# Sliding-window attention in 36 batches of four tiles that run across head groups, and column sums over partitions on GpSimd, in a gated mix of two attention blocks

## The chip, the cores and the metric

The kernel runs on one core of one Trainium2 chip. The metric is the device time of one execution in microseconds. Each run of a kernel has several executions; a median is quoted with the number of them. The profile is one execution of each kernel; its span is a little shorter than the measured time of the same execution (491.1 against 492.9 us for the kernel before).

Engine names: PE is the tensor engine (matmuls), PEld its weight loads, DVE is VectorE, ACT is ScalarE, POOL is GpSimd, SP issues most DMA; a q behind a name (SPq) is that engine's instruction queue. PSUM is the memory that the matmuls here write, bank by bank (a projection fills one bank with 128x512 fp32 values), and to evacuate a bank is to copy it to SBUF, where the program keeps its other tiles. The granted clock is the share of full speed that the profile shows for PE.

## The reference, cut to what matters

Two attention blocks read the same `x` (2048 x 1024, bf16), with 32 heads of 32, and a per-row gate mixes their outputs.

```python
# A: linear attention
pq, pk = phi(q), phi(k)                         # phi(t) = where(t > 0, t + 1, exp(t)) + 1e-6
kv = einsum("bhsd,bhse->bhde", pk, v)
z  = einsum("bhsd->bhd", pk)                    # column sums of A's keys over the 2048 rows
o  = einsum("bhqd,bhde->bhqe", pq, kv) / (einsum("bhqd,bhd->bhq", pq, z)[..., None] + 1e-6)
# B: each row attends to 8 keys, at distances 0, 2, ... 14
logits = where(mask, q . k[pos - 2 * w] * Dh ** -0.5, -1e9);  attn = softmax(logits)
# mix
g = sigmoid((x * gate_w).sum(-1));  out = g * A(x) + (1 - g) * B(x)
```

## The kernel before: the parts that the change and the argument touch

The rows are kept as even rows, then odd rows, so a distance of 2 becomes a distance of 1. In program order PE does: key projection of A (`pk_ps`); `G = x^T pk` (`g_ps`); `kv = Wv^T G` per head group (`kv_ps`) and the column sums (`z_ps`); value projection of B and query projection of A in turn (the "V stage", `p_ps`); then for each of 8 groups of four heads the key and query projection of B (`kq_ps`), with the window attention of the group before woven in; a rest of the query projection of A (`q_ps`); and the output projections (`q_ps`, `d_ps`). PE's order is the program's; the `interleave` helper sets the attention pieces between the projection matmuls.

Column sums: VectorE adds the 16 row tiles of `pk` into `zacc`, alternating with the 16 products for the gate; then `zacc` is split into a high and a low bf16 part, and matmuls with a matrix of ones sum both over the partitions.

```python
def side(t):                                   # called once per finished 128x512 piece of G
    if t:
        nc.vector.tensor_tensor(out=zacc[:], in0=zacc[:] if t > 1 else pk[:, 0, :], in1=pk[:, t, :], op=ALU.add)
    nc.vector.tensor_tensor_reduce(out=zhl[:, 0, :], in0=xrow[:, t, :], in1=gw_row[:], ..., accum_out=gdot[:, t:t + 1])
# [cut]
nc.vector.tensor_copy(out=zhl[:, 0, :], in_=zacc[:])
nc.vector.tensor_tensor(out=zhl[:, 1, :], in0=zacc[:], in1=zhl[:, 0, :], op=ALU.subtract)
# [cut: the kv matmuls]
for half in range(2):
    zp = ps_1.tile([P, 512], F32, name="z_ps", tag="p1")
    for i in range(2):
        nc.tensor.matmul(zp[:], lhsT=onesb[:], rhs=zhl[:, i, half * 512:(half + 1) * 512], start=(i == 0), stop=(i == 1))
    nc.scalar.copy(out=zrow[:, half * 512:(half + 1) * 512], in_=zp[:])
```

Window attention: the 2048 queries of a head group are 18 tiles of 112 or 128 queries, each against 128 keys. A batch is three or four tiles of one head group: 4, 4, 4, 3, 3 for seven groups, and six batches of three for the last, 41 in all. Scores use only the 32 rows of one head, so four heads run side by side as 32-row tiles.

```python
for q0, w, k0 in tiles:                        # scores of one batch
    for i in range(4):
        r = slice(32 * i, 32 * i + 32)
        nc.tensor.matmul(s4[:, i, o:o + w], lhsT=kqt[r, 0, k0:k0 + P], rhs=kqt[r, 1, q0:q0 + w], ...)
    o += w
for h in range(2):                             # two exponentials and two masks for a batch
    nc.scalar.activation(out=ptv[:, hs], in_=s4[:, hs, 0:W_], func=ACT.Exp, scale=SCALE)
    nc.vector.tensor_tensor(out=ptv[:, hs], in0=ptv[:, hs], in1=m[...], op=ALU.mult)
# later, after a lag: 4 value matmuls of 33 columns per tile, reciprocal, multiply, DMA transpose
```

## Time and profile before

| kernel before | value |
|---|---|
| time, median of 3 / of 6 executions | 493.66 us / 493.7 us |
| PE busy | 481.1 of 491.1 us |
| VectorE, ScalarE, GpSimd busy | 58%, 37%, 2% |
| 128x512 matmul: printed / real step | 379 ns / 0.216 us |

The first lines are from the page of the kernel before: the busy time of each engine with its share of the span and its number of instructions, and the shares of the chain that ended last by engine.

```profile
PE 481.1 (98%) x3276; PEld 230.0 (47%) x3336; DVE 282.8 (58%) x548; ACT 180.6 (37%) x279; POOL 7.6 (2%) x26
PE 91%; SPq 5%; DMA 2%; issue 1%; DVE 0%; ACT 0%; ACTq 0%
```

PE is almost always busy and almost the whole chain. What PE doesn't execute can only matter if PE waits for it. So PE's waits come next, for the kernel before: who waited for whom, us in total, times, the longest. "issue" stands for idle time in which the profile shows nothing that PE waited for.

```profile
PE kq_ps L338 <- issue: 1.3, 8, 0.2
PE warm L163 <- DVE onesb L116: 1.1, 1, 1.1
PE pk_ps L157 <- DMA WkA_75<-in_A_wqkv_dram: 0.7, 1, 0.7
PE pk_ps L157 <- DMA xT<-in_A_x_dram: 0.4, 1, 0.4
PE pk_ps L157 <- DMA WkA_96<-in_A_wqkv_dram: 0.3, 1, 0.3
PE q_ps L295 <- issue: 0.3, 2, 0.2
```

The third view is the PE timeline of the kernel before: start, duration, the instruction, its shapes and how many were merged. These lines are the boundaries: start of `kv_ps`, of the ones-matmuls, of the V stage, of attention and of the main output projection.

```profile
117.81 1.95 PE L220 MATMUL kv_ps<-G_624,WvA_102 128*128 128x128 bf16 x32
121.38 1.03 PE L227 MATMUL z_ps<-zhl,onesb 128*128 128x512 bf16 x3
122.25 1.03 PE L261 MATMUL p_ps<-WvB_110,xT 128*128 128x512 bf16 x4
222.39 1.89 PE L338 MATMUL kq_ps<-xT,WkB_1039 128*128 128x512 bf16 x8
384.23 1.89 PE L457 MATMUL d_ps<-WoA_106,pqT_4054 128*128 128x512 bf16 x8
```

A duration includes the tail of a pipelined matmul that overlaps the next, so one reads starts and not durations: from `z_ps` to `p_ps` is 0.87 us, which is four steps of 0.216 (only three of the four records are in the trace). From `kq_ps` to `d_ps`, the attention stretch, is 161.84 us.

### The profile page before, as it was taken

The numbers are of one execution on the slowest core, as the hardware profiler recorded it, in microseconds if no ns is written. First come the engines' busy times: TensorE is split into PE (matmuls) and PEld (weight loads), VectorE is DVE, ScalarE is ACT, GpSimd is POOL, SyncE is SP. The second block draws the span as 40 slices with busy tenths as digits, with TensorE's granted clock in tenths as the row PEclk, the third lists the DMA queues.
The fourth block names the chain that finished last, engine by engine and source line by source line (L and its number), as shares of the span: only waits on it lengthen the run. The fifth ranks groups of instructions, "written<-read, shape, count | busy, mean of one in ns | idle before, by whom it ended". The sixth has DMA issues, their size and how long they took to land.

```text
span 491.1 us, 8153 instructions
## 1 busy us (share of the span) xinstructions
PE 481.1 (98%) x3276; PEld 230.0 (47%) x3336; DVE 282.8 (58%) x548; ACT 180.6 (37%) x279; POOL 7.6 (2%) x26
## 2 busy tenths in 40 slices
PE   8999999999999999999999999999999999999997
PEld 5444444446444444444445444444544444444444
DVE  1666669951329999997476767676765496000000
ACT  2333321112543333332555555655565333112121
POOL 3000000000200000000000000000000000000000
PEclk9999999999999999999999999999999999999999
DMA  8999950001521222235011133111174933010101
GB/s 195 173 297 368 348 183 0 0 1 44 177 76 54 86 94 92 73 135 173 4 34 30 32 96 54 26 36 37 29 136 90 217 87 84 35 43 33 43 34 43
DMA packets 80309, 46.56 MB, mean 95 GB/s; under 512 B 53648, under 2 KB 74256, under 8 KB 80272
## 3 DMA queue, kind: packets, MB, share of 16 engines
q1 hardware_dynamic: 80272, 46.04, 34.4%
q8 instruction: 26, 0.43, 0.4%
q14 instruction: 11, 0.09, 0.1%
HBM read 21.23 MB, written 7.34 MB: 58 GB/s over the span
## 4 chain that ended last, share of the span: by engine, by line
PE 91%; SPq 5%; DMA 2%; issue 1%; DVE 0%; ACT 0%; ACTq 0%
PE kq_ps L338 23%; PE d_ps L457 21%; PE g_ps L202 11%; PE p_ps L261 11%; PE p_ps L295 8%; PE pk_ps L157 6%; SPq L104 4%; PE q_ps L295 2%; DMA WkA_96<-in_A_wqkv_dram 2%; PE kv_ps L220 1%; PE q_ps_4355 L457 1%; PE p_ps L250 1%; PE q_ps L457 1%; SPq L101 0%; PE q_ps_4236 L295 0%
## 5 line engine op out<-in xcount | busy, mean ns | idle before, releaser
L202 PE MATMUL g_ps<-pk,xrow 128*128 128x512 bf16 x251 | 55.2, 379 | 0.3
L145 DVE TENSOR_SCALAR e<-e 128x512 f32<-128x512 f32 x64 | 27.2, 425 | 42.7 <-ACT e L144 42.7
L462 ACT ACTIVATE osb<-d_ps,omg 128x512 bf16<-128x512 f32 (+1 forms) x31 | 20.9, 673 | 74.5 <-PE d_ps L457 68.7
L157 PEld LDWEIGHTS <-xT 128*128 128x128 bf16 x256 | 24.9, 98 | 32.5 <-issue 1.5
L457 PEld LDWEIGHTS <-OBT 128*128 128x128 bf16 x264 | 25.8, 98 | 29.2
L202 PEld LDWEIGHTS <-xrow 128*128 128x128 bf16 x256 | 25.0, 98 | 30.2
L261 PEld LDWEIGHTS <-xT 128*128 128x128 bf16 x256 | 25.0, 98 | 30.2
L295 PEld LDWEIGHTS <-xT 128*128 128x128 bf16 x256 | 24.2, 98 | 28.0
L144 ACT ACTIVATE e<-pk_ps 128x512 f32<-128x512 f32 x32 | 19.0, 597 | 42.3 <-PE pk_ps L157 33.2
L377 DVE TENSOR_TENSOR PT_1863<-PT_1863,mask 128x672 bf16<-128x672 bf16 (+3 forms) x42 | 23.7, 571 | 17.9 <-ACT PT_1863 L375 17.4
L338 PE MATMUL kq_ps<-xT,WqB_1846 128*128 128x512 bf16 x120 | 31.8, 379 | 1.0 <-issue 0.6
L338 PE MATMUL kq_ps<-xT,WqB_1844 128*128 128x512 bf16 x124 | 31.7, 379 | 0.7 <-issue 0.5
L377 DVE TENSOR_TENSOR PT_1864<-PT_1864,mask 128x672 bf16<-128x672 bf16 (+3 forms) x40 | 22.3, 565 | 17.0 <-ACT PT_1864 L375 16.5
L338 PE MATMUL kq_ps<-xT,WkB_1041 128*128 128x512 bf16 x122 | 31.6, 379 | 0.2
L344 DVE CAST kqt<-kq_ps 128x512 bf16<-128x512 f32 x32 | 22.0, 687 | 16.5 <-PE kq_ps L338 16.5
L338 PE MATMUL kq_ps<-xT,WkB_1039 128*128 128x512 bf16 x120 | 30.7, 379 | 0.4 <-issue 0.2
L261 PE MATMUL p_ps<-WvB_112,xT 128*128 128x512 bf16 x126 | 30.6, 379 | 0.1
L261 PE MATMUL p_ps<-WvB_110,xT 128*128 128x512 bf16 x125 | 30.6, 379 | 0.1
L266 ACT CAST tmp<-p_ps 128x512 bf16<-128x512 f32 x32 | 18.8, 588 | 30.2 <-PE p_ps L261 27.9
L457 PEld LDWEIGHTS <-pqT_4413 128*128 128x128 bf16 x200 | 19.6, 98 | 22.1
L157 PE MATMUL pk_ps<-WkA_75,xT 128*128 128x512 bf16 x125 | 28.1, 380 | 1.4 <-DMA WkA_75<-in_A_wqkv_dram 0.7
L457 PE MATMUL d_ps<-WoB_4050,OBT 128*128 128x512 bf16 (+1 forms) x126 | 28.3, 365 | 0.1
(393 smaller groups left out, 665.8 us busy)
## 6 DMA issues: line engine op xcount, KB each, us to landing
xrow<-in_A_x_dram SPq DMA_DIRECT2D x4, 1024.0 KB, 13.0
out_dram<-osb SPq DMA_DIRECT2D x31, 128.0 KB, 1.9
pqd<-tmp SPq DMA_DIRECT2D x12, 256.0 KB, 2.0
V<-tmp SPq DMA_DIRECT2D x4, 264.0 KB, 2.4
WkA_75<-in_A_wqkv_dram SPq DMA_DIRECT2D x4, 256.0 KB, 3.8
WkA_96<-in_A_wqkv_dram SPq DMA_DIRECT2D x1, 1024.0 KB, 8.5
WvA_102<-in_A_wqkv_dram SPq DMA_DIRECT2D x1, 1024.0 KB, 15.3
WvA_104<-in_A_wqkv_dram SPq DMA_DIRECT2D x1, 1024.0 KB, 14.7
```

Source lines behind the costliest of these rows:

```text
L104: nc.sync.dma_start_transpose(out=xT[:, :, t * P:(t + 1) * P], in_=rows(x, t * P, (t + 1) * P))
L144: nc.scalar.activation(out=e[:], in_=pj[:], func=ACT.Exp)
L145: nc.vector.tensor_scalar(out=e[:], in0=e[:], scalar1=1.0, scalar2=1e-6, op0=ALU.min, op1=ALU.add)
L157: nc.tensor.matmul(pj[:], lhsT=xT[:, kt, t * P:(t + 1) * P], rhs=WkA[half][:, kt, :], start=(kt == 0), stop=(kt == KT - 1))
L202: nc.tensor.matmul(pj[:], lhsT=xrow[:, t, kt * P:(kt + 1) * P], rhs=pk[:, t, half * 512:(half + 1) * 512], start=(t == 0), stop=(t == NB - 1))
L261: nc.tensor.matmul(st["pj"][:], lhsT=xT[:, kt, t * P:(t + 1) * P], rhs=WvB[half][:, kt, :], start=(kt == 0), stop=(kt == KT - 1))
L295: nc.tensor.matmul(st["pj"][:], lhsT=xT[:, kt, t * P:(t + 1) * P], rhs=WqA[half][:, kt, :], start=(kt == 0), stop=(kt == KT - 1))
L338: nc.tensor.matmul(st["pj"][:], lhsT=W[c // 4][:, kt, (c % 4) * P:(c % 4 + 1) * P], rhs=xT[:, kt, cols], start=(kt == 0), stop=(kt == KT - 1))
L344: nc.vector.tensor_copy(out=kqt[:, 1, cols], in_=st["pj"][:])
L377: nc.vector.tensor_tensor(out=ptv[:, hs], in0=ptv[:, hs], in1=m[:, None, :].broadcast_to([P, 2, W_]), op=ALU.mult)
L457: nc.tensor.matmul(st["ps"][:, 0:n], lhsT=lhsT, rhs=W[c0 // 512][:, c, c0 % 512:c0 % 512 + n], start=(side == 0 and c == 0), stop=(side == ...
L462: nc.scalar.activation(out=osb[:, 0:n], in_=st["ps"][:, 0:n], func=ACT.Copy, scale=omg[:, tb:tb + 1])
```

## The change

The intent: fewer and always equal attention batches, so that what a batch costs in itself is paid 36 times and not 41; and no PE work for the column sums. Supporting changes: the K or Q evacuation goes to VectorE when it falls just behind a batch's scores (ScalarE has exponentials to do then) and to ScalarE otherwise; VectorE does all adds first, so that the all-reduce can start early; and the projections in the last attention stretch lose a third PSUM bank, since each batch now needs both banks of the value matmuls.

```diff
-            def side(t):
-                if t:
-                    nc.vector.tensor_tensor(out=zacc[:], ... op=ALU.add)
-                nc.vector.tensor_tensor_reduce(out=zhl[:, 0, :], ... accum_out=gdot[:, t:t + 1])
+            side = []
+            for t in range(1, NB):
+                side.append(lambda t=t: nc.vector.tensor_tensor(out=zacc[:], ... op=ALU.add))
+            side.append(lambda: nc.gpsimd.partition_all_reduce(zrow[:], zacc[:], P, bass_isa.ReduceOp.add))
+            for t in range(NB):
+                side.append(lambda t=t: nc.vector.tensor_tensor_reduce(out=gjunk[:], ... accum_out=gdot[:, t:t + 1]))
 [cut: called two at a time; the bf16 split, the ones-matmuls and the zrow copies go]
-                        if which == 0:
-                            nc.scalar.copy(out=kqt[:, 0, cols], in_=st["pj"][:])
-                        else:
-                            nc.vector.tensor_copy(out=kqt[:, 1, cols], in_=st["pj"][:])
+                        after = (64 * c + 16 * b + 8 * which + 8 - 67) % (512 / 36)
+                        (nc.vector.tensor_copy if 0 <= after < 4 else nc.scalar.copy)(
+                            out=kqt[:, which, cols], in_=st["pj"][:])
-                GROUPS = [QT[a:b] for a, b in zip(cuts, cuts[1:])]      # batches within one head group
+            TILES = [(c, t) for c in range(KT) for t in range(18)]
+            state = [dict() for _ in range(len(TILES) // 4)]            # 36 batches across head groups
+            for g in range(len(state)):
+                p_ = 64 + 3 + 512 * g / len(state)
+                events.append((p_, lambda g=g: scores(g)))
+                events.append((p_ + 18, lambda g=g: pv(g)))
 [cut: masks for a 128-query tile in any place; bank8 (three banks) becomes bank2 (two)]
```

## The prediction

> **What bounds the kernel.** The tensor engine. The page gives PE 481.1 us busy of 491.1 (98%) at full granted clock; the chain of waits is 91% PE, and PE's own waits sum to about 4 us: 1.3 us "issue" in the K/Q projections, 1.1 us before the warm-up, 1.1 us for first loads, 0.3 us for the second half of Wk. VectorE has 58%, ScalarE 37%, GpSimd 2%. Only what PE executes, or a new wait, can count.
>
> **Terms on PE (PE timeline).** A 128x512 matmul advances the stream by 0.216 us (its printed 379 ns overlaps its neighbours).
> 1. Column sums: four ones-matmuls go (121.38 to 122.25): -0.87 us.
> 2. Batches: 41 (seven heads of 5, one of 6) become 36; the 144 tiles stay. The value part is linear in tiles (0.41 us for four, 0.31 for three): no gain. The score part takes about 0.39 us for four and 0.34 for three, so about 0.2 us of a batch is fixed: 5 x 0.2 = -1.0 us.
> 3. 0.16 us "issue" gaps recur behind some three-tile batches, some ten in all. Those batches vanish; I count half: -0.5 us.
> 4. In the last attention stretch projections have two PSUM banks, not three, all evacuated by ScalarE, whose pair of exponentials now always takes 1.8 us (1.35 for three tiles), where eight matmuls take 1.73. One or two short bank waits: +0.3 us.
>
> **Off the critical path.** Ten fewer exp and ten fewer mask instructions (fixed parts only, about 1.5 us on each engine), zrow copies (1.07 us ScalarE), the bf16 split of the sums (1.85 us VectorE). About 14 K/Q evacuations move from VectorE (0.69 us) to ScalarE (0.59 us). VectorE's busy time falls by some 13 us, ScalarE's rises by some 5; no effect on time.
>
> **The GpSimd sum.** The 15 VectorE adds, 1.14 us apart, now run first: 64.5 to 82 us. The all-reduce follows. Its result is first read at about 148 us, but GpSimd executes in order, and behind it stand two PT fills (1.66 us each) and the ones columns of V staging, which the first V transfers need at about 127 us and whose two buffers hold ScalarE from about 133. So about 45 us are free. The Trainium skill, "GPSIMD Engine Reference", Cross-partition, gives 247.7 us for a partition-axis reduce of 128x2048; by columns an estimated 124 us here, which would cost some 65 us. No run here shows it, and it is another instruction; I expect 10 to 40 us, hidden. The same page (Instruction dispatch) gives about 6 us for a routine's first call: hidden. Loading it adds DMA traffic in the first 35 us, where DMA is saturated and PE already waits for Wk: +0.3 us.
>
> **Sum.** -0.87 - 1.0 - 0.5 + 0.3 + 0.3 = -1.8 us: 491.9 us; 8 in 10 between 489.8 and 494.5. Chances: faster by over 2% 0.02, within 0.90, slower 0.08.
>
> **What would show it.** No z matmuls, V beginning 0.9 us sooner after G ends. 36 score batches; attention (first K/Q matmul to first d_ps matmul, 161.7 us before) about 160.5. PE waits still about 4 us, none on GpSimd; the first multiply by zrow not waiting for it. The all-reduce over before 125 us on the GpSimd timeline.
>
> **What would make it wrong.** An all-reduce over 50 us (GpSimd busy past 130 us, V transfers and ScalarE waiting, PE stalled for banks); early loads delayed by the routine's own transfer; bank or exponential waits at every batch (36 x 0.05 us would cancel everything).

## The result, and the profile after

The changed kernel took 491.62 us (median of 6, 490.83 to 492.64) against 493.7 us (median of 6, 492.6 to 494.39), ratio 0.9964 with a 95% interval of 0.9945 to 0.9983. A second set of 6 gave 491.2 us and 0.9962 (0.9947 to 0.9977). A ratio is the mean time of one kernel's fast runs over that of the other's of the same rounds, so it is not quite the ratio of the medians quoted. The gain is real and small: about 1.8 us, 0.4%.

The same lines of the page of the changed kernel:

```profile
PE 484.8 (99%) x3332; PEld 230.5 (47%) x3332; DVE 279.1 (57%) x512; ACT 188.4 (38%) x283; POOL 16.0 (3%) x33
PE 98%; DMA 1%; SPq 0%; ACT 0%; issue 0%; ACTq 0%
```

PE's busy time is higher although it does less: more of its records are in this trace (3332 matmul records against 3276, with four fewer executed). Busy time can't settle a change of 2 us here. PE's waits of the changed kernel and the boundaries from its PE timeline can:

```profile
PE warm L162 <- DVE onesb L114: 1.1, 1, 1.1
PE pk_ps L156 <- DMA WkA<-in_A_wqkv_dram: 0.9, 2, 0.7
PE pk_ps L156 <- DMA xT<-in_A_x_dram: 0.8, 1, 0.8
```

```profile
119.33 3.74 PE L220 MATMUL kv_ps<-G,WvA 128*128 128x128 bf16 x64
122.90 1.03 PE L254 MATMUL p_ps<-WvB,xT 128*128 128x512 bf16 x4
223.05 1.89 PE L331 MATMUL kq_ps<-xT,WkB 128*128 128x512 bf16 x8
383.82 1.89 PE L444 MATMUL d_ps<-WoA,pqT 128*128 128x512 bf16 x8
```

The differences of starts, for every profiled run (columns in us; "first" is from the first key projection to `g_ps`, read from the same view; "att" is the attention stretch; "output" is from the first `d_ps` to the end of the span, which is printed to 0.1 us):

| run | first | G | kv to V | V stage | att | output |
|---|---|---|---|---|---|---|
| before | 56.75 | 55.25 | 4.44 | 100.14 | 161.84 | 106.87 |
| changed, first profile | 58.25 | 55.25 | 3.57 | 100.15 | 160.77 | 107.08 |
| changed, again | 57.58 | 55.25 | 3.58 | 100.15 | 160.77 | 107.13 |
| sums alone | 57.05 | 55.25 | 3.57 | 100.15 | 161.83 | 106.90 |
| batches alone | 56.36 | 55.26 | 4.43 | 100.15 | 160.76 | 107.07 |
| batches of three | 56.22 | 55.25 | 3.57 | 100.15 | 163.36 | 107.37 |
| scores split | 57.39 | 55.25 | 3.58 | 100.14 | 168.61 | 107.07 |
| five all-reduces early | 57.76 | 55.25 | 12.45 | 100.15 | 160.77 | 107.07 |
| five all-reduces late | 57.72 | 55.25 | 3.58 | 111.26 | 160.77 | 107.11 |
| start rearranged | 56.13 | 55.25 | 3.58 | 100.14 | 160.77 | 107.09 |
| routine loaded, unused | 57.13 | 55.25 | 4.44 | 100.14 | 161.84 | 106.86 |
| K/Q evacuation as before | 56.55 | 55.26 | 3.57 | 100.14 | 161.18 | 107.11 |

Every stage but the first repeats to some hundredths from run to run when nothing in it was changed. This table resolves what the times can't. The change shows in two columns: -0.87 us (kv to V) and -1.07 us (attention), together -1.94 us, against 0.0036 to 0.0038 of about 493 us, which is 1.8 to 1.9 us. A third column goes the other way: "output" is about 0.2 us longer in every kernel with the new batches (107.07 to 107.37) than in the three with the old ones (106.86 to 106.90). PE has no part in it, as from the first start of `d_ps` to the last printed one are 102.76 us in both kernels; the difference lies behind ScalarE's last evacuation, and nothing here shows its cause. With it the stages give about -1.7 us. The first stage scatters by 2 us; in the first profile of the changed kernel the granted clock was 0.79 between 8 and 16 us, in the second 1.00.

GpSimd's timeline of the changed kernel, behind the masks:

```profile
84.97 6.99 POOL L191 PARTITION_ALL_REDUCE zrow<-zacc  x1 [71.50 <-DVE zacc L189]
109.30 3.28 POOL L322 MEMSET PT<- 128x1872 bf16 x2 [17.34 <-issue]
119.56 0.38 POOL L232 MEMSET tmp<- 128x32 bf16 x2 [6.97 <-PE g_ps L204]
```

The all-reduce takes 7.0 us and is over at 92 us, far ahead of 149.16 us, where VectorE first multiplies by its result. But VectorE's timeline at that moment, again of the changed kernel, shows a neighbour that suffers:

```profile
84.75 1.22 DVE L193 CUSTOM_DVE_ANT_0 gjunk<-xrow,gw_row 128x1024 bf16<-128x1024 bf16 x1
86.01 5.43 DVE L193 CUSTOM_DVE_ANT_0 gjunk<-xrow,gw_row 128x1024 bf16<-128x1024 bf16 x1
91.49 1.23 DVE L193 CUSTOM_DVE_ANT_0 gjunk<-xrow,gw_row 128x1024 bf16<-128x1024 bf16 x1
109.47 1.52 DVE L213 TENSOR_SCALAR ratio<-ratio 128x16 f32<-128x16 f32 x1 [0.28 <-ACT ratio L212]
```

The gate product that starts beside the all-reduce takes 5.43 us in place of 1.22, so it was held up by 4.2 us; it ends at 91.44 us, half a microsecond before the printed end of the all-reduce (spans on GpSimd are rough). The product before it, which began 0.2 us before the all-reduce, was not slowed. The tiny operation on `ratio` beside GpSimd's fill takes 1.52 us; in the kernel before it took 0.17. The Trainium skill, "SBUF — State Buffer", Who interferes with whom, says that a VectorE instruction with two SBUF inputs contends with a GpSimd instruction that reads SBUF, and that the loser is blocked for the whole instruction. The gate product has two such inputs, and the trace agrees in kind: a hold of 4.2 us beside an all-reduce of 7.0. The sentence does not cover `ratio`, which has one input beside a fill that only writes; what held that up, no run here isolates. Nothing waited for it here, as G's matmuls kept PE busy until 119 us.

VectorE's busy time fell by 3.7 us and ScalarE's rose by 7.8 us. In attention VectorE fell by 11.3 us (104.3 to 92.9, read by stretch), but in the G stage it rose (39.2 to 46.9), for these blocked instructions count as busy.

### The profile page after: what moved, and what is told of

Same layout as the page of the kernel before. It is cut to its first block, busy times and chain, and to the rows that moved or that the text cites. A ratio compares the mean times of both kernels' runs of the same rounds, so it can differ in the third digit from the quotient of the medians.

```text
span 490.9 us, 8143 instructions
## 1 busy us (share of the span) xinstructions
PE 484.8 (99%) x3332; PEld 230.5 (47%) x3332; DVE 279.1 (57%) x512; ACT 188.4 (38%) x283; POOL 16.0 (3%) x33
## 4 chain that ended last, share of the span: by engine, by line
PE 98%; DMA 1%; SPq 0%; ACT 0%; issue 0%; ACTq 0%
PE kq_ps L331 23%; PE d_ps L444 21%; PE pk_ps L156 11%; PE g_ps L204 11%; PE p_ps L254 11%; PE p_ps L288 8%; PE q_ps L288 3%; PE oB L382 3%; PE s L357 2%; PE q_ps L444 1%; DMA xT<-in_A_x_dram 1%; PE kv_ps L220 1%; PE p_ps L243 1%; SPq L95 0%; SPq L99 0%; ACT osb L449 0%
## 5 line engine op out<-in xcount | busy, mean ns | idle before, releaser
L367 ACT ACTIVATE PT<-s 128x896 bf16<-128x896 f32 (+1 forms) x72 | 63.0, 926 | 24.5 <-PE s L357 24.5
L331 PE MATMUL kq_ps<-xT,WkB 128*128 128x512 bf16 x256 | 65.3, 379 | 0.0
L331 PE MATMUL kq_ps<-xT,WqB 128*128 128x512 bf16 x256 | 64.8, 379 | 0.0
L368 DVE TENSOR_TENSOR PT<-PT,mask 128x896 bf16<-128x896 bf16 (+1 forms) x72 | 44.7, 624 | 26.6 <-ACT PT L367 26.5
L156 PE MATMUL pk_ps<-WkA,xT 128*128 128x512 bf16 x256 | 57.4, 387 | 1.7 <-DMA WkA<-in_A_wqkv_dram 0.9
L254 PE MATMUL p_ps<-WvB,xT 128*128 128x512 bf16 x256 | 58.5, 379 | 0.0
L444 PE MATMUL d_ps<-WoA,pqT 128*128 128x512 bf16 (+1 forms) x248 | 56.9, 372 | 0.0
L444 PE MATMUL d_ps<-WoB,OBT 128*128 128x512 bf16 (+1 forms) x248 | 56.9, 372 | 0.0
L288 PE MATMUL p_ps<-WqA,xT 128*128 128x512 bf16 x192 | 43.4, 379 | 0.0
L336 ACT CAST kqt<-kq_ps 128x512 bf16<-128x512 f32 x48 | 28.2, 588 | 31.8 <-PE kq_ps L331 31.6
```

The source lines that it names most:

```text
L156: nc.tensor.matmul(pj[:], lhsT=xT[:, kt, t * P:(t + 1) * P], rhs=WkA[half][:, kt, :], start=(kt == 0), stop=(kt == KT - 1))
L254: nc.tensor.matmul(st["pj"][:], lhsT=xT[:, kt, t * P:(t + 1) * P], rhs=WvB[half][:, kt, :], start=(kt == 0), stop=(kt == KT - 1))
L288: nc.tensor.matmul(st["pj"][:], lhsT=xT[:, kt, t * P:(t + 1) * P], rhs=WqA[half][:, kt, :], start=(kt == 0), stop=(kt == KT - 1))
L331: nc.tensor.matmul(st["pj"][:], lhsT=W[c // 4][:, kt, (c % 4) * P:(c % 4 + 1) * P], rhs=xT[:, kt, cols], start=(kt == 0), stop=(kt == KT - 1))
L336: (nc.vector.tensor_copy if 0 <= after < 4 else nc.scalar.copy)(out=kqt[:, which, cols], in_=st["pj"][:])
L444: nc.tensor.matmul(st["ps"][:, 0:n], lhsT=lhsT, rhs=W[c0 // 512][:, c, c0 % 512:c0 % 512 + n], start=(side == 0 and c == 0), stop=(side == ...
```

## The experiments

### Each half of the change alone

Sums alone: the kernel before with the new `side` list, the all-reduce, and no bf16 split, ones-matmuls or `zrow` copies. Batches alone: the changed kernel with these parts taken back. Both are compared with the changed kernel run again in the same rounds.

```diff
 # sums alone, on the kernel before
-  nc.tensor.matmul(zp[:], lhsT=onesb[:], rhs=zhl[...])      # and all that belongs to it
+  side.append(lambda: nc.gpsimd.partition_all_reduce(zrow[:], zacc[:], P, bass_isa.ReduceOp.add))
 # batches alone, on the changed kernel: the same lines the other way round
```

> The changed kernel itself, as the mark for the other runs. It should repeat 491.6 us (ratio 0.996), and its early slices show whether the low granted clock of the first profile of it (0.79 between 8 and 16 us) belongs to the change or to one execution: I expect full clock, and then a profiled span 1 to 2 us below 490.9.

> The kernel before with the column sums on GpSimd alone (and the sums reordered on VectorE for it); batches as before. My theory: only the four ones-matmuls leave PE, so -0.9 us, 492.8 us, V stage beginning 0.87 us sooner after the end of G, attention stretch unchanged at 161.7 us. Rival: the whole gain comes from elsewhere (batches) or the loading of the GpSimd routine costs as much as the matmuls save: 493.7 us.

> The changed kernel with the column sums by ones-matmuls again: 36 batches alone. My theory: a fixed part of about 0.2 us of each of five batches, so -1.0 to -1.5 us, 492.3 us, attention stretch about 160.8 us as in the changed kernel. Rival: batches are free and the column sums give it all: 493.7 us.

Measured: kernel before 492.67 us (median of 11); changed 491.2 us, ratio 0.9962 (0.9947 to 0.9977), at full clock as expected, but with a span of 490.3 us, only 0.6 below the first profile where 1 to 2 were expected; sums alone 491.99 us, 0.9979 (0.9961 to 0.9997); batches alone 491.92 us, 0.9978 (0.9963 to 0.9992). Each half gives about half, and 0.0021 and 0.0022 add to 0.0043, against 0.0038 together, within the intervals. By stage it is exact: sums alone has 3.57 and 161.83 us, batches alone 4.43 and 160.76 us. Both rivals, that one half gives everything, fall.

### What a batch costs PE: more batches, and more switches with the same batches

Two runs ask why five batches fewer save 1.07 us. The first cuts the same 144 tiles in 48 batches of three.

```diff
-            state = [dict() for _ in range(len(TILES) // 4)]
+            state = [dict() for _ in range(len(TILES) // 3)]
 [cut: 4 becomes 3 where a batch is cut, evacuated and transposed; the period of the evacuation rule is 512 / 48]
```

> The changed kernel with 48 batches of three tiles in place of 36 of four; the same 144 tiles, the same matmuls. My theory of a fixed PE cost per batch of about 0.2 us: 12 more batches, +2.4 us, 494.0 us, attention stretch about 163.2 us, no new waits of PE. Rival: the cost goes by tiles, and five batches fewer gave nothing in themselves: 491.6 us.

Measured: 493.72 us, ratio to the kernel before 1.0014 (0.9999 to 1.0029); attention 163.36 us. Twelve batches more cost 163.36 - 160.77 = 2.59 us, 0.216 us each; five fewer saved 1.07 us, 0.214 us each. The cost goes by batches.

The second run keeps the 36 batches with their exponentials, masks and banks, and only issues the 16 score matmuls in two lots, with two projection matmuls between.

```diff
-                events.append((p_, lambda g=g: scores(g)))
+                events.append((p_ - 2, lambda g=g: scores(g, 0)))     # first two tiles
+                events.append((p_, lambda g=g: scores(g, 1)))         # other two, then exp and mask
```

> The changed kernel with the 16 score matmuls of a batch issued in two places, two tiles each, two projection matmuls apart; the exponentials, masks, banks and waits of a batch stay one set. Theory 1: the 0.215 us that a batch costs PE beyond its tiles is the change between full-height matmuls (128 rows) and the four 32-row tiles, so 36 more changes cost 36 x 0.215 = 7.7 us: attention stretch 168.5 us, about 499 us. Rival: it is what a batch waits for (its bank, its semaphores), and splitting costs nothing: 160.8 us, 491.5 us.

Measured: 499.66 us, ratio 1.013 (1.0108 to 1.0152); attention 168.61 us, so 36 more places cost 7.84 us, 0.218 us each. These are lines from its PE timeline:

```profile
240.22 0.28 PE L359 MATMUL s<-kqt 32*128 32x112 bf16 x8
240.43 0.60 PE L331 MATMUL kq_ps<-xT,WkB 128*128 128x512 bf16 x2
240.97 0.28 PE L359 MATMUL s<-kqt 32*128 32x112 bf16 x8
241.18 0.82 PE L331 MATMUL kq_ps<-xT,WkB 128*128 128x512 bf16 x3
```

From one `s` to the next is 0.75 us, of which two projection matmuls take 0.43. The other 0.32 us is for 8 small matmuls; with 16 in one place, 14 projection matmuls and one set of value matmuls (0.41 us), a batch period of the changed kernel is 3.84 us, which leaves 3.84 - 3.02 - 0.41 = 0.41 us for 16. So 8 more matmuls cost 0.09 us, and the place itself about 0.23, near the 0.218 of the table. The column `32*128` against `128*128` names what differs: scores use 32-row tiles of the array, everything around them all 128 rows. The Trainium skill, "TensorEngine Tiling (Array Packing)", Key Properties, says that changing the tiling mode, not just the tile, drains TensorE. The three measurements (0.214, 0.216, 0.218 us for each way there and back) agree with it in kind; the page gives no figure. The rival, that a batch costs what it waits for, falls: the split added no exponential, mask, bank or evacuation, and PE's list of waits for this run has only the start (1.1 us and 0.7 us). The value matmuls speak for the tile height and against a mere interruption of a projection: they interrupt it too, at full height, and cost 0.41 us for four tiles and 0.31 us for three, in proportion to the tiles with nothing fixed. The weight loads (PEld timelines of both kernels) add a hint: the first one for the value matmuls begins 0.21 us before them, behind the last projection matmul, while the first one for the scores begins only with the first score matmul (median 0.00 us). Whether the 0.215 us is this lost overlap or something else that goes with the switch is not shown; what happens inside the array, no trace shows.

### The "issue" gaps of the prediction

No kernel was needed. The second profile of the changed kernel has six "issue" gaps of 0.16 us in attention; the first has none; both stretches are 160.77 us. These are the same three steps from the PE timelines of the first and of the second profile:

```profile
252.78 0.38 PE L357 MATMUL s<-kqt 32*128 32x112 bf16 x16
253.10 1.04 PE L331 MATMUL kq_ps<-xT,WqB 128*128 128x512 bf16 x4
253.97 0.56 PE L382 MATMUL oB<-V,PT 128*128 128x33 bf16 x16
```

```profile
252.13 0.38 PE L357 MATMUL s<-kqt 32*128 32x112 bf16 x16
252.67 0.81 PE L331 MATMUL kq_ps<-xT,WqB 128*128 128x512 bf16 x3 [0.16 <-issue]
253.32 0.56 PE L382 MATMUL oB<-V,PT 128*128 128x33 bf16 x16
```

Both take 1.19 us from `s` to `oB`. Where the gap is printed, one of the four matmuls has no record: the gap is the place of the missing record, and PE was working.

### Is the all-reduce hidden, and by how much?

> The changed kernel with the all-reduce issued five times in a row (same result), from about 84 us. By the GpSimd queue alone (what the prediction counted) it would end near 120 us, the ones columns near 124, and cost nothing. Rival: GpSimd and VectorE exclude each other on it, as the one 5.4 us gate product beside the all-reduce suggests; then the gate products (16 of them, two SBUF inputs each) are pushed back by some 4 x 6 us, from 109 to about 133 us, ScalarE waits for them with the G copies behind, and PE stalls at the KV matmuls from about 119: about +15 us, 507 us.

> The same five all-reduces, but VectorE does the gate products first and the adds after, so that the all-reduces run from about 103 us beside instructions with one SBUF input at most. Exclusion of GpSimd and VectorE can then cost nothing; only the GpSimd queue counts: end near 138, ones columns near 142 in place of the 127 where they are needed. I expect +2 to +6 us by ScalarE waiting for its V staging buffers, that is 493 to 497 us, well under the early five. If exclusion is not the cause, this one is slower than the early five.

```diff
 # early five
-  side.append(lambda: nc.gpsimd.partition_all_reduce(zrow[:], zacc[:], P, bass_isa.ReduceOp.add))
+  side.append(lambda: [nc.gpsimd.partition_all_reduce(zrow[:], zacc[:], P, bass_isa.ReduceOp.add) for _ in range(5)])
 # late five: the same, and the 16 gate products stand before the 15 adds in the list
```

Measured, early five: 501.2 us, ratio to the kernel before 1.0162 (1.0144 to 1.0179), about 10 us more than the changed kernel. Lines from its GpSimd, VectorE (the first two of the ten gate products that alternate so) and PE timelines:

```profile
84.70 33.94 POOL L191 PARTITION_ALL_REDUCE zrow<-zacc  x5 [71.50 <-DVE zacc L189]
85.74 5.43 DVE L193 CUSTOM_DVE_ANT_0 gjunk<-xrow,gw_row 128x1024 bf16<-128x1024 bf16 x1
91.22 1.23 DVE L193 CUSTOM_DVE_ANT_0 gjunk<-xrow,gw_row 128x1024 bf16<-128x1024 bf16 x1
126.53 5.15 PE L220 MATMUL kv_ps<-G,WvA 128*128 128x128 bf16 x56 [6.86 <-ACT G L207]
```

GpSimd ended at 118.64 us, which the prediction's "about 45 us are free" would call free. But beside each of the five one gate product took 5.43 us in place of 1.22, and the next one 1.22 again. The gate products ended near 126 us (109 in the changed kernel; the four further holds of 4.2 us are 16.8), ScalarE waited 23.2 us for them with five copies of G behind, and PE waited 6.86 us for those copies. The mechanism is the rival's; its size was overestimated (126 us in place of 133, and 10 us in place of 15).

The stretch grew by 12.45 - 3.57 = 8.88 us, more than the wait. The rest is the clock. This view of the early five gives, for four stretches, the length, PE's busy time with its matmuls in brackets, the granted PE clock, DMA share and GB/s:

```profile
120.00:122.00 2.00, 0.00 (x0) 1.00 0.00 0
124.00:126.00 2.00, 0.00 (x0) 0.50 0.00 0
128.00:130.00 2.00, 2.00 (x21) 0.50 0.00 0
132.00:136.00 4.00, 4.00 (x20) 1.00 1.08 361
```

After some 4 us without matmuls the granted clock fell to half, and it stayed there for some 4 us after the work came back. The Trainium skill, "TensorE: Matmul & The Clock Gate", What's actually happening, states half clock after an idle window of about 3.4 us and full clock after about as much sustained work; the trace agrees for the fall, while the return took 3.9 us here and 5.5 us in the late five. Half of that, 2.0 and 2.8 us, is what the two stages lost beyond PE's wait.

Late five: 503.45 us, ratio 1.0211 (1.0193 to 1.0229). All gate products took 1.22 us; the five all-reduces took 30.97 us (6.2 each; VectorE had no instruction with two SBUF inputs beside them), from 106.90 to 137.87 us. The ones columns came at 141.5 us where the first V transfer needs them at about 127. ScalarE waited 11.1 us for that transfer, PE 8.3 us for ScalarE, and the V stage grew by 11.1 us, again with the clock at 0.50 from about 140 us. I expected 2 to 6 us. The queue's limit is real and lies where the prediction put it, but passing it by 14 us costs most of that. My line that a late five slower than the early five would clear exclusion was badly set: it is slower, and yet the traces show two different causes, one in each run. The totals alone would have misled.

### The loading of the routine

In every trace with the all-reduce, GpSimd does nothing from about 1.3 us to 8.3-9.7 us; in the two without it there is no such pause. This run adds a one-column all-reduce to the kernel before, and nothing else.

```diff
+            tiny = junk.tile([P, 2], F32, name="tiny", tag="tiny")
+            nc.vector.memset(tiny[:], 1.0)
+            nc.gpsimd.partition_all_reduce(tiny[:, 0:1], tiny[:, 1:2], P, bass_isa.ReduceOp.add)
```

> The kernel before with a one-column all-reduce on GpSimd whose result nobody uses: it adds the loading of the routine at the start (in the traces so far GpSimd stands still for 7.1 to 7.8 us from about 1.3 us wherever the routine is used, and not where it isn't), and nothing else. If loading delays the first weights and rows on the DMA queues, the stage up to G grows from 56.4-56.8 us to 57-58 us as in most traces with the routine, and the time by 0.3 to 0.9 us. Rival: that stage scatters by itself; time 492.9 us, ratio 1.000 within 0.001.

Measured: 493.21 us against 493.36 us, ratio 0.9994 (0.9978 to 1.001). This line of its GpSimd timeline shows the pause:

```profile
8.32 1.46 POOL L127 TENSOR_SCALAR_AFFINE_SELECT mask<-mask 128x128 bf16<-128x128 bf16 x6 [7.06 <-issue]
```

The Trainium skill, "GPSIMD Engine Reference", Instruction dispatch, states some 6 us for the first call of a freshly loaded kernel. The pause of 7.1 us is of that size, but it comes at the first mask operation and not at the all-reduce, which at one column took 0.40 us at 65 us. That the pause is the loading is inferred. A cost in time isn't shown: the first stage was 57.13 us, and the interval leaves no more than 0.1% (0.5 us). Whether a small part of the scatter of the first stage belongs to it stays open.

### K/Q evacuation as before

```diff
-                        after = (64 * c + 16 * b + 8 * which + 8 - 67) % (512 / 36)
-                        (nc.vector.tensor_copy if 0 <= after < 4 else nc.scalar.copy)(
+                        (nc.vector.tensor_copy if which else nc.scalar.copy)(
```

> The changed kernel with K evacuated by ScalarE and Q by VectorE again, in place of the choice by the distance to the last scores. My theory: PE never waits for either, so the attention stretch stays at 160.8 us and the time at 491.2 us. Rival: with batches of four every time, the longer exponentials hold up K's evacuation and with it one of two PSUM banks, and the new choice is what hides that: attention stretch 161.5 us or more.

Measured: 491.42 us, ratio 0.9962 (0.9946 to 0.9978), the same as the changed kernel in time; attention 161.18 us, in between the two expectations. So the choice is worth 0.41 us, which only the stage table shows: three batch periods are 3.96 us in place of 3.84, though PE's list of waits names no wait for it. In each of the three, PE begins a query projection 0.05 us after VectorE has ended its copy of the Q before (258.76 after 258.71, 293.90 after 293.85, 329.04 after 328.99 us), which stood behind two masks on VectorE; with two banks in turn, the bank that PE needs is the one of that Q. So my theory that PE never waits is a little wrong. The rival expected 0.7 us and got the engine wrong: the bank was held by Q's evacuation on VectorE, not by K's behind the exponentials on ScalarE. The new choice of engine kept these waits from taking back part of the 5 x 0.215 us that the batches saved.

### Failed: a rearranged start

The traces have 0.7 to 2.5 us of waits of PE for first loads. A candidate to beat both kernels sends the first half of Wk from ScalarE's queue beside SP's transposes, moves the second half up, and orders the key projection so that rows of x are needed later.

```diff
-        nc.sync.dma_start(out=WkA[0][:, 2 * i:2 * i + 2, :], ...)
+        nc.scalar.dma_start(out=WkA[0][:, 2 * i:2 * i + 2, :], ...)
-            for half in range(2):
-                for t in range(NB):
+            for ts, half in ((range(2, 8), 0), (range(8), 1), (range(8, NB), 0), (range(8, NB), 1)):
+                for t in ts:
```

> A candidate to beat both: the changed kernel with the first Wk half sent from the ScalarE queue beside the transposes of x on SP, the second half moved up behind the eighth transpose, and the key projection in the order tiles 2-7 half 0, 0-7 half 1, 8-15 half 0, 8-15 half 1, so that x is needed later. First full projection near 5.3 us with no gap of 1 to 2 us behind it: stage from first projection to G 55.5 us in place of 56.2 to 58.3, time 490.0 us. Rival: the transposes are limited by DMA, so the start gains and the middle loses the same: 491.3 us.

Measured: 492.24 us, ratio to the kernel before 0.9979 (0.9959 to 0.9999), no better than the changed kernel (0.9964 and 0.9962). PE's longest wait is now for x itself:

```profile
PE pk_ps L154 <- DMA xT<-in_A_x_dram: 1.7, 2, 1.3
```

The first projection started at 6.44 us in place of 5.8, since the first transpose landed no earlier, and the first stage, 56.13 us, is only as good as the best of the others. The wait moved from Wk to x. What would bring the first transpose in earlier is open.

A version of the changed kernel with the third PSUM bank in the last stretch is not on record as a run. By the author's account it doesn't build, for a projection that holds that bank in mid-sum stands in PE's order before the value matmuls that need the same bank (a deadlock).

## Why the prediction was right

- **What bounds the kernel: right.** PE is the chain, and only the two PE terms show in time.
- **Column sums, -0.87 us: right**, to the hundredth (4.44 to 3.57 us).
- **Batches, -1.0 us: right in mechanism and size.** Measured -1.07 us, 0.214 us per batch; the runs with 48 batches and with split scores give 0.216 and 0.218 us and tie it to the places where 32-row tiles stand, which the prediction did not name.
- **"Issue" gaps, -0.5 us: wrong.** They are missing records of matmuls. The kernel before could have told: its batches of three with and without a printed gap are equally long.
- **Bank waits in the last stretch, +0.3 us: not there.** Attention changed by five batches' worth and nothing else, and the batch periods of the last stretch (3.84 and 3.85 us) are those of the others. That a late evacuation could hold PE up was not baseless: with the old rule it costs 0.41 us over the whole stretch, but by VectorE and not by ScalarE.
- **Loading the routine, +0.3 us: not shown.** 0.9994 (0.9978 to 1.001). The last three terms were together +0.1 us, so the sum of -1.8 us was right partly by luck: a wrong -0.5 met two +0.3 that did not come, and the 0.2 us behind PE's end was not foreseen.
- **The all-reduce hides: right; its length: too pessimistic.** 7.0 us in place of 10 to 40. The estimate of 124 us from the skill's figure for another instruction would have been 18 times too long.
- **"About 45 us are free": wrong in this order of work.** The prediction counted GpSimd's queue and not that VectorE's gate products are held up meanwhile. Five all-reduces, 34 us, already cost 10 us.
- **Busy times: half right.** ScalarE +7.8 us (predicted +5), VectorE -3.7 us (predicted -13): blocked VectorE instructions count as busy. No effect on time, as said.

## What to carry to other kernels

When one engine is 98% busy, cost a change by start-to-start steps of that engine's stream and compare stages by the starts at their borders; here that resolves hundredths of a microsecond, where times resolve about one and busy sums mislead. Each excursion from full-height matmuls to 32-row tiles and back cost PE about 0.215 us here, one 128x512 matmul: gather small-tile matmuls into as few places as the PSUM banks allow. An instruction on GpSimd was free here as long as nobody waited for the two-input SBUF work of VectorE beside it (early five) and GpSimd's queue came free in time (late five).

## What the Trainium skill lacked or had wrong

- "TensorEngine Tiling (Array Packing)", Key Properties: says that a change of mode drains, without a cost. Here 0.214 to 0.218 us for each way to four 32-row tiles and back.
- "GPSIMD Engine Reference", Cross-partition: its only time is 247.7 us for a partition-axis `tensor_reduce` of 128x2048. `partition_all_reduce` of 128x1024 fp32 took 6.99 us, 6.2 us each in a row undisturbed, and 0.40 us for one column.
- "GPSIMD Engine Reference", Instruction dispatch: some 6 us at the first call. Here the pause was 7.0 to 8.5 us, and it stood before the first mask operation, some 57 to 99 us ahead of the all-reduce.
- "SBUF — State Buffer", Who interferes with whom: agrees in kind. What it doesn't say is how it looks in a profile: the VectorE instruction that is held up is shown as busy for 5.43 us in place of 1.22, and ends 0.5 us before the printed end of the all-reduce.
- No page that was used here says that printed "issue" gaps of 0.16 us in a PE stream can be missing records of matmuls: the same steps took 1.19 us with and without such a gap.
